# A two-layer decode kernel: which part of w2 is loaded last, what stays in memory between the layers, and the block order at the turn

## The chip, the cores and the metric

One core of one Trainium2 chip runs the whole kernel, in float32. The metric is the time of one execution on the device in microseconds (us); lower is better. The engines of the core work side by side: TensorE (PE, with its weight loads PEld) multiplies, VectorE (DVE) and ScalarE (ACT) work on single elements, SyncE (SP) issues nearly all the transfers from the chip's main memory (HBM) into the on-chip memory, and 16 DMA engines carry them out. A transfer of 128 rows is shared by the 16 DMA engines, and counts as landed when the last of them is done with its part.

## The reference

```python
def A(x, k_cache, v_cache, wq, wo):            # attention over a cache, 8 sequences, one new token each
    q = (x @ wq) as 32 heads of 128            # wq 1024 x 4096
    k, v = caches of 4 heads x 4096 x 128      # each one serves 8 query heads
    p = softmax(q @ k.T * 128 ** -0.5)
    return (p @ v as 4096 columns) @ wo        # wo 4096 x 1024

def B(x, w1, b1, w2, b2):                      # w1 1024 x 3584, w2 3584 x 1024
    return gelu(x @ w1 + b1) @ w2 + b2

for layer in range(2):                         # the same weights and caches in both layers
    x = x + A(layernorm(x), ...)
    x = x + B(layernorm(x), ...)
```

x is 8 x 1024. The caches are 64 MB each (8 MB of K and 8 MB of V for one sequence), wq and wo 16 MB each, w1 and w2 14 MB each. Both layers need all of it, and the on-chip memory holds only a part.

## The kernel before

The on-chip buffer, the arena, is 52 units of 0.5 MB (`SCW` = 1024 columns of 128 rows each, 4 bytes). A list `stream` holds all loads in the order in which SP issues them, each with its size in units and the unit at which it starts, all written out by hand. `pump` issues loads from the head of the list as long as their units are free; `release` frees units and calls `pump`. A load that has to wait holds back all those behind it. In the program, the load waits for the last instruction that reads its units.

The order of the work in a layer: the query product (wq), then for each sequence K (scores, in 8 pieces of 1 MB), softmax, V (8 pieces of 1 MB), then wo, a layernorm, w1 with gelu (7 groups of 512 hidden columns, `expand`), and w2. Layer 0 takes the sequences 0 to 7, layer 1 takes them 7 to 0, so the last V pieces of sequence 7 can stay in the arena from one layer to the next (`n_kept`). wq stays in the arena during the whole attention of layer 0 (all but its last row block, which is parked elsewhere, in part in `spare`, and comes back with `unpark`; a small rest is loaded again as "qe").

**The turn** from layer 0 to layer 1 is `swap`. w2 is cut into column blocks (`W2_PARTS`). For one block, `down` multiplies all 28 row blocks of 128 hidden columns (28 x 2 TensorE passes, since a float32 matmul is issued as two), VectorE copies the sum, small matmuls turn it (L511), and the result is added to x. These columns of x then are the rows by which wq is multiplied for the next layer (`q_part`, 8 passes for each 1 MB of wq). Used wq tiles free their units, and w2's next blocks and the first K pieces of layer 1 go there. So the chain is: w2 block, copy, wq parts, release, next load. Most of w2 stays in the arena for layer 1, except for its last four row blocks (`LAST` = 24 and on): of these two column blocks of 256 stay, and the other two are loaded again.

**The end** is layer 1's `expand` with `work`: after each group of w1 the product with the w2 rows of the group before is done (`grow`, `down_row`). The last four row blocks need the last group of w1. The list ends with w1's pieces (five of 2 MB, three of 1 MB, then 0.5, 0.25 and 0.25 MB) and the two column blocks of the last four rows of w2, 1 MB, in five parts (`LATE`); one part is cut into rows (`ROWS`), so the last seven transfers have 16 to 256 KB. After the last matmul, VectorE adds the sum to x (L835), and SP stores x.

Of the kernel before, what the change touches and what calls it, by code (L numbers as in the profile page):

```python
# [38 lines left out]
UNPARK = 14  # L39
# [8 lines left out]
LATE_ORDER = [(e, c) for e in range(4) for c in range(CB)]  # L48
# [60 lines left out]
def decode_layers(ctx: ExitStack, tc: tile.TileContext, x, kc, vc, wq, wo, w1, w2, out):  # L109
# [145 lines left out]
    def pump():  # L255
        while stream:
# [8 lines left out]
            for r0, r1 in ROWS.get(key, ((0, P),)):  # L265
                nc.sync.dma_start(out=slot.ap[r0:r1, 0:src.shape[1]], in_=src[r0:r1])
# [18 lines left out]
    def expand(name, rs, work=None):  # L285
        n = 0
        for slot in tiles((name,)):
# [23 lines left out]
            release(slot)  # L311
            if n % NT:
                continue
            if u < WIDE:
                row = row_s if work or u % 2 else qz[:, P:P + CH]
                nc.scalar.activation(row, acc, AF.Copy, scale=rs)
                if not work:
                    flush()
                pending.append(lambda u=u, row=row: hidden_wide(u, row))
            else:  # L320
                if not work:
                    flush()
                row, hid = row_s[:, 0:P], qz[:, P:2 * P]
                if direct:
                    row = acc[:, 0:P]
                else:
                    nc.scalar.activation(row, acc[:, 0:P], AF.Copy, scale=rs)
                nc.vector.transpose(hid, row)
                hv = hid.rearrange("p (t q) -> p t q", t=GT)[:, :, 0:B]
                if biased:  # L330
                    hidden_group(u, None, hv)
                else:
                    hidden_group(u, lambda pre: nc.vector.tensor_tensor(pre, hv, bias1(u), ALU.add))
            for f in (work or {}).get(u, ()):
                f()
# [15 lines left out]
    def q_part(acc, u, kt, c0, ap):  # L351

        n = ap.shape[1]
        for j in range(4):
            d0, d1 = max(c0, j * CH), min(c0 + n, (j + 1) * CH)
            if d0 < d1:
                nc.tensor.matmul(acc[u][32 * j:32 * j + 32, d0 - j * CH:d1 - j * CH], xnT[:, kt * XS:kt * XS + 32],  # L357
                                 ap[:, d0 - c0:d1 - c0], start=(kt == 0), stop=(kt == NT - 1 and d1 == (j + 1) * CH))
# [4 lines left out]
    def queries(rs):  # L363
        acc = q_acc()
        at = 0
        for slot in tiles(("q0",)):
            for c in range(0, slot.cols, W):
                q_part(acc, at % 2, at // 2, 0, slot.ap[:, c:c + W])
# [94 lines left out]
    def down_row(y, kts, cs=range(CB)):  # L463

        for kt in kts:
            for c in cs:
                nc.tensor.matmul(y[32 * c:32 * c + 32], h_at(kt), w2_at[c, kt], start=(kt == 0), stop=(kt == NFT - 1))  # L467

    def w2_kts(c, i):

        k0, n, _ = W2_PARTS[c][i]
        return range(k0, k0 + n)

    def arrive(key, kts):
        slot = held[key]
        for e, kt in enumerate(kts):
            w2_at[key[1], kt] = slot.ap[:, e * Q4:(e + 1) * Q4]
        return kts

    def swap():  # L480
# [8 lines left out]
        def used(kt, u):  # L489
# [3 lines left out]
            if (kt, u) == (4, 0):  # L493
                st["unparked"] = unpark()

        for c in range(CB):
            y = ys[:, c % 2 * Q4:(c % 2 + 1) * Q4]
# [5 lines left out]
            slot = held.pop(("w2", c, [k0 for k0, _, _ in W2_PARTS[c]].index(LAST)))  # L503
            if c < len(LATE_AT):
                release(slot)
            ysb = row_s[:, c % 2 * Q4:(c % 2 + 1) * Q4]
# [3 lines left out]
            for i in range(2):  # L510
                nc.tensor.matmul(pt[:, i * B:(i + 1) * B], ysb[:, i * P:(i + 1) * P], bsel, start=True, stop=True)  # L511
            xc = xv[:, 2 * c:2 * c + 2]
# [396 lines left out]
```

## Time and profile before

| | before |
|---|---|
| median of 3 runs | 849.92 us (849.53 to 849.97) |
| the profiled execution | 849.15 us |
| span from first to last instruction in it | 847.4 us |
| read from HBM | 357.78 MB, 422 GB/s over the span |
| TensorE busy | 520.4 us (61%) |
| VectorE busy | 203.1 us (24%) |
| mean granted TensorE clock | 0.813 |

How to read the rows: the page gives busy shares in 40 equal slices, DMA among them; the chain of work that ended last gives, in order of time, a start, a duration and what was at work. Rows of windows give for a stretch its length, then busy time and number of instructions for PE, PEld, DVE, ACT and POOL, then the granted clock, the busy share of the DMA engines and GB/s. Rows of the timeline give start, time, engine, line, operation, output and inputs, shape and count; in brackets, how long the engine had been idle and what ended that.

### The profile page before, as it was taken

The numbers are of one execution on the slowest core, as the hardware profiler recorded it, in microseconds if no ns is written. First come the engines' busy times: TensorE is split into PE (matmuls) and PEld (weight loads), VectorE is DVE, ScalarE is ACT, GpSimd is POOL, SyncE is SP. The second block draws the span as 40 slices with busy tenths as digits, with TensorE's granted clock in tenths as the row PEclk, the third lists the DMA queues.
The fourth block names the chain that finished last, engine by engine and source line by source line (L and its number), as shares of the span: only waits on it lengthen the run. The fifth ranks groups of instructions, "written<-read, shape, count | busy, mean of one in ns | idle before, by whom it ended". The sixth has DMA issues, their size and how long they took to land.

```text
span 847.4 us, 9420 instructions
## 1 busy us (share of the span) xinstructions
PE 520.4 (61%) x4060; PEld 173.3 (20%) x4060; DVE 203.1 (24%) x692; ACT 55.5 (7%) x118; POOL 2.4 (0%) x14
## 2 busy tenths in 40 slices
PE   0756565655656656655678775476646565665777
PEld 0211111111111111122143222121111111112334
DVE  0013141322223131300120242231413222231022
ACT  0110000000000000000211100000000000000021
POOL 0000000000000000000000000000000000000000
PEclk9977788786887868688889988877896878788689
DMA  9999999999999999999999999999999999999997
GB/s 402 420 421 432 433 422 439 427 431 435 419 429 436 428 438 417 429 428 425 427 410 413 424 428 432 432 433 426 437 427 435 429 434 430 427 435 426 423 426 260
DMA packets 20073, 358.52 MB, mean 423 GB/s; under 512 B 2240, under 2 KB 2880, under 8 KB 4416
## 3 DMA queue, kind: packets, MB, share of 16 engines
q1 hardware_dynamic: 19888, 357.77, 99.2%
q8 instruction: 32, 0.52, 0.3%
q10 hardware_dynamic: 144, 0.15, 0.1%
q14 instruction: 9, 0.07, 0.0%
HBM read 357.78 MB, written 0.13 MB: 422 GB/s over the span
## 4 chain that ended last, share of the span: by engine, by line
DMA 75%; PE 21%; DVE 2%; issue 1%; another core or an unknown queue 1%; ACT 0%; SPq 0%; ACTq 0%; DVEq 0%
DMA arena<-in_k_dram 29%; DMA arena<-in_v_dram 21%; DMA arena<-in_w_dram 11%; DMA arena<-in_wo_dram 8%; PE sps L590 8%; PE o_ps L633 7%; DMA arena<-in_wq_dram 5%; PE y L424 1%; PE acc L357 1%; PE sps L461 1%; PE sps L645 1%; PE acc L301 1%; PE sps L467 0%; ACT sps L614 0%
## 5 line engine op out<-in xcount | busy, mean ns | idle before, releaser
L590 PE MATMUL sps<-arena,qz 128*32 128x512 f32 x1024 | 161.9, 775 | 118.5 <-DMA arena<-in_k_dram 117.4
L633 PE MATMUL o_ps<-arena 128*32 128x512 f32 x512 | 84.2, 788 | 51.1 <-DMA arena<-in_v_dram 39.6
L633 PE MATMUL o_ps<-arena,spare 128*32 128x512 f32 x512 | 85.3, 785 | 45.9 <-DMA arena<-in_v_dram 41.3
L590 PEld LDWEIGHTS sps<-arena,qz 128*32 128x32 f32 x1024 | 36.8, 132 | 208.6 <-issue 170.0
L638 DVE SCALAR_TENSOR_TENSOR scr<-o_ps,bits,scr 128x128 f32<-128x128 f32 x192 | 67.4, 351 | 6.8
L424 PE MATMUL y<-arena,oxT 128*32 128x256 f32 x512 | 42.5, 494 | 28.5 <-DMA arena<-in_wo_dram 28.5
L636 DVE TENSOR_SCALAR scr<-o_ps,bits 128x128 f32<-128x128 f32 x64 | 22.4, 351 | 150.4 <-PE o_ps L633 150.4
L645 PEld LDWEIGHTS sps<-bits,scr 128*128 128x128 f32 x128 | 22.3, 219 | 69.5 <-issue 46.9
L357 PE MATMUL acc<-arena,oxT 128*32 128x512 f32 x248 | 30.5, 630 | 6.0 <-DMA arena<-in_wq_dram 4.6
L633 PEld LDWEIGHTS o_ps<-arena 128*32 128x32 f32 x512 | 16.3, 131 | 83.0 <-issue 47.7
L301 PE MATMUL acc<-arena,oxT 128*32 128x512 f32 x160 | 25.5, 760 | 12.6 <-DMA arena<-in_w_dram 12.6
L633 PEld LDWEIGHTS o_ps<-arena,spare 128*32 128x32 f32 x512 | 17.6, 131 | 76.4 <-issue 51.1
L595 DVE TENSOR_SCALAR_CACHE_REDUCE arena<-sps 128x512 f32<-128x512 f32 x16 | 11.1, 692 | 88.9 <-PE sps L590 88.9
L646 DVE TENSOR_TENSOR oxT<-sps,scr 128x8 f32<-128x8 f32 x64 | 10.6, 165 | 88.9 <-PE sps L645 88.9
L595 DVE TENSOR_SCALAR_CACHE_REDUCE spare<-sps 128x512 f32<-128x512 f32 x16 | 11.1, 692 | 80.8 <-PE sps L590 80.8
L614 ACT ACTIVATE sps<-arena,bits 128x512 f32<-128x512 f32 x16 | 10.9, 681 | 284.3 <-DVE scr L608 284.3
L424 PEld LDWEIGHTS y<-arena,oxT 128*32 128x32 f32 x512 | 19.2, 138 | 49.7 <-DMA arena<-in_wo_dram 28.7
L614 ACT ACTIVATE sps<-spare,bits 128x512 f32<-128x512 f32 x16 | 10.9, 681 | 268.9 <-DVE scr L608 268.9
L645 PE MATMUL sps<-bits,scr 128*128 128x8 f32 x128 | 28.2, 293 | 0.0
L604 PE MATMUL sps<-scr,bits 128*128 128x128 f32 x32 | 7.6, 322 | 22.9 <-DVE scr L600 22.9
L461 PE MATMUL sps<-arena,oxT 128*32 128x256 f32 x224 | 15.0, 409 | 3.8 <-DMA arena<-in_w_dram 3.8
L203 PE MATMUL sps<-ident,xb 128*128 128x128 f32 x6 | 1.5, 345 | 24.4 <-DMA xb<-in_x_dram 23.3
(136 smaller groups left out, 251.1 us busy)
## 6 DMA issues: line engine op xcount, KB each, us to landing
arena<-in_v_dram SPq DMA_DIRECT2D x25, 4096.0 KB, 20.6
arena<-in_k_dram SPq DMA_DIRECT2D x21, 4096.0 KB, 21.0
arena<-in_k_dram SPq DMA_DIRECT2D x20, 2048.0 KB, 18.8
arena<-in_w_dram SPq DMA_DIRECT2D x16, 2048.0 KB, 11.8
arena<-in_v_dram SPq DMA_DIRECT2D x11, 2048.0 KB, 20.2
arena<-in_wo_dram SPq DMA_DIRECT2D x8, 2048.0 KB, 16.1
arena<-in_wo_dram SPq DMA_DIRECT2D x3, 4096.0 KB, 23.9
arena<-in_w_dram SPq DMA_DIRECT2D x6, 1024.0 KB, 19.0
```

Source lines behind the costliest of these rows:

```text
L301: nc.tensor.matmul(acc[32 * j:32 * j + 32, :], lhs, slot.ap[:, c:c + CH], start=(kt < 4), stop=(kt >= NT - 4))
L357: nc.tensor.matmul(acc[u][32 * j:32 * j + 32, d0 - j * CH:d1 - j * CH], xnT[:, kt * XS:kt * XS + 32], ap[:, d0 - c0:d1 - c0], start=(kt == ...
L424: nc.tensor.matmul(y[32 * j:32 * j + 32, 0:Q4], lhs[:, n * B:n * B + 32], slot.ap[:, c + j * Q4:c + (j + 1) * Q4], start=(n == 0), stop=(n ...
L461: nc.tensor.matmul(y[32 * g:32 * g + 32], h_at(kt), w2_at[c, kt], start=(n < 4), stop=(n >= NFT - 4))
L590: nc.tensor.matmul(ps[32 * g:32 * g + 32, :], qz[:, c:c + 32], kt[:, g * CH:(g + 1) * CH], start=(j == 0), stop=(j == HKV - 1))
L595: nc.vector.tensor_scalar(st["row", b].ap[:, half * CH:(half + 1) * CH], ps, SCALE, None, op0=ALU.mult, op1=ALU.max, accum_out=st["mx", b] ...
L614: nc.scalar.activation(pp, row[:, h * CH:(h + 1) * CH], AF.Exp, bias=bias, scale=1.0, accum_out=ls[:, h:h + 1])
L633: nc.tensor.matmul(o[32 * g:32 * g + 32, :], s[:, g], v[:, g * CH:(g + 1) * CH], start=(half == 0), stop=(half == NH - 1))
L636: nc.vector.tensor_scalar(r, o[:, 0:P], sel_t[:, 0:1], None, op0=ALU.mult)
L638: nc.vector.scalar_tensor_tensor(r, o[:, t * P:(t + 1) * P], sel_t[:, t:t + 1], r, op0=ALU.mult, op1=ALU.add)
L645: nc.tensor.matmul(po[:, 0:REP], r_s[j % 2], sel_h, start=True, stop=True)
L646: nc.vector.tensor_tensor(oT_v[:, j * REP:(j + 1) * REP, b], po[:, 0:REP], rl_s[b % 2][:, j * REP:(j + 1) * REP], ALU.mult)
```

## The change

- The four last row blocks of w2 all are loaded again at the end: 2 MB in three transfers of 1, 0.5 and 0.5 MB (row blocks 24 and 25, then 26, then 27, all 1024 columns each). They lie in a copy behind w2's image in HBM.
- Seven pieces of the last V (7 MB) stay between the layers, not six. The buffer for wo and w1 in layer 0 is units 42 to 51, and the first loads of layer 1 go to units 16 to 27 (before: 40 to 51 and 14 to 27). The last V of layer 0 comes in transfers of 1, 3 and 4 MB.
- At the turn w2 comes in five column blocks: 128, 256, 256, 256 and 128 columns (`BLOCKS`, in units of 128 columns from column block 0, 2, 4, 6 and 1). wq's row blocks are stored and used in the order `ORDER`, so that the row block that was parked (now 1) belongs to the last column block. In layer 1 the first quarter of the columns therefore is in two pieces, and `down_row` makes two matmuls of 128 columns there where it made one of 256.
- w1's pieces in layer 1 are six of 2 MB and two of 1 MB. `expand` can take pieces that hold one group's end and the next one's start, which layer 0 needs for its pieces of 2, 2 and 1 MB.
- In one V transfer of sequence 1 in layer 1 (4 MB) the last 64 columns are left out and come in five transfers of 96, 12, 10, 6 and 4 rows (`CUTS`). `ROWS` is gone.

```diff
-UNPARK = 14
+UNPARK = 16
-W2_PARTS = (((0, 16, 40), (16, 8, 44), (LAST, 4, 46)), ((0, 4, 47), (4, 16, 48), (20, 4, 46), (LAST, 4, 0)),
-            ((LAST, 4, 1), (0, 16, 2), (16, 8, 6)), ((LAST, 4, 0), (0, 16, 8), (16, 8, 12)))
-LATE_AT = 14, 15
-LATE = ((0, 0, 2), (1, 0, 2), (0, 2, 2), (1, 2, 1), (1, 3, 1))
-ROWS = {("late", 0, 0): ((0, 8), (8, 16), (16, P))}
+ORDER = [0, 2, 3, 4, 5, 6, 7, 1]
+BLOCKS = ((0, 1), (2, 2), (4, 2), (6, 2), (1, 1))
+W2_PARTS = (((0, 24, 42), (LAST, 4, 45)),
+            ((16, 8, 50), (0, 16, 46), (LAST, 4, 45)),
+            ((0, 16, 0), (LAST, 4, 45), (16, 8, 4)),
+            ((0, 16, 6), (16, 8, 10), (LAST, 4, 45)),
+            ((0, 24, 12), (LAST, 4, 15)))
+LATE = ((0, 2, 15), (2, 1, 17), (3, 1, 45))
+CUTS = {(1, ("v", 1, 2, 0)): ((0, 96), (96, 108), (108, 118), (118, 124), (124, 128))}
...
-            for r0, r1 in ROWS.get(key, ((0, P),)):
-                nc.sync.dma_start(out=slot.ap[r0:r1, 0:src.shape[1]], in_=src[r0:r1])
+            n = src.shape[1]
+            full = n - P // 2 if key in CUTS else n
+            nc.sync.dma_start(out=slot.ap[:, 0:full], in_=src[:, 0:full])
+            for r0, r1 in CUTS.get(key, ()):
+                nc.sync.dma_start(out=slot.ap[r0:r1, full:n], in_=src[r0:r1, full:n])
...
             for c in cs:
-                nc.tensor.matmul(y[32 * c:32 * c + 32], h_at(kt), w2_at[c, kt], start=(kt == 0), stop=(kt == NFT - 1))
+                at = 0
+                for i, w in W2_OF[c] if kt < LAST else ((c, Q4),):
+                    nc.tensor.matmul(y[32 * c:32 * c + 32, at:at + w], h_at(kt), w2_at[i, kt],
+                                     start=(kt == 0 and at == 0), stop=(kt == NFT - 1))
+                    at += w
...
-        for c in range(CB):
-            y = ys[:, c % 2 * Q4:(c % 2 + 1) * Q4]
+        for c, (k0, nk) in enumerate(BLOCKS):
+            w = nk * P
+            y = ys[:, c % 2 * Q4:c % 2 * Q4 + w]
...
-            for kt in (2 * c, 2 * c + 1):
+            for kt in range(k0, k0 + nk):
...
-    n_kept = 6
+    n_kept = 7
...
+    batch(0, last_b, ((8, 28), (4, 36), (4, 40)), ((2, 44), (6, 28), (8, 34)))
-    weights(("o0",), wo[0], [4, 4, 2, 2, 4, 4, 4, 4, 4], fixed(40, 44, 48, 50, 40, 44, 48, 40, 44))
-    weights(("i0",), w1[0], [4] * 7, fixed(48, 40, 44, 48, 40, 44, 48))
+    weights(("o0",), wo[0], [4, 4, 2] * 3 + [2], fixed(*[46, 42, 50] * 3, 46))
+    weights(("i0",), w1[0], [4, 4, 2, 4, 4, 2, 4, 4], fixed(42, 46, 50, 42, 46, 50, 42, 46))
...
-    batch(1, last_b, ((4, 16), (4, 20), (4, 24), (2, 14), (2, 16)), ((4, 20),))
-    batch(1, last_b - 1, ((4, 24), (4, 16), (2, 14), (4, 20), (2, 36)), ((8, 28), (8, 16)))
-    batch(1, last_b - 2, ((4, 36), (4, 24), (8, 28)), ((8, 16), (8, 24)))
-    at = [32, 16, 24] * (4 * B)
+    batch(1, last_b, ((2, 18), (4, 20), (4, 24), (2, 16), (2, 18), (2, 20)), ((2, 22),))
+    batch(1, last_b - 1, ((4, 24), (4, 16), (4, 20), (4, 28)), ((8, 34), (8, 18)))
+    at = [26, 34, 18] * (4 * B)
...
-    weights(("i1",), w1[0], [4] * 5 + [2] * 3 + [1, 0.5, 0.5], fixed(32, 36, 16, 20, 24, 28, 30, 32, 34, 35, 36))
-    for c, e, n in LATE:
-        at = (c * NFT + LAST + e) * Q4
-        to = LATE_AT[c] * SCW + e * Q4
-        stream.append((("late", c, e), 0 if e else 1, w2[0][:, at:at + n * Q4], arena.ap[:, to:to + n * Q4] if e else (LATE_AT[c],), ()))
+    weights(("i1",), w1[0], [4] * 6 + [2] * 2, fixed(34, 38, 18, 22, 26, 30, 34, 36))
+    for e, n, at in LATE:
+        c0 = W2_FROM[-1] + e * D
+        stream.append((("late", e), n, w2[0][:, c0:c0 + n * D], (at,), ()))
...
-            for c, e, n in LATE:
-                arrive(("late", c, e), range(LAST + e, LAST + e + n))
-            for e, c in LATE_ORDER:
-                grow((LAST + e,), (c,))
+            for e, n, _ in LATE:
+                slot = held[("late", e)]
+                for i in range(n):
+                    for c in range(CB):
+                        w2_at[c, LAST + e + i] = slot.ap[:, i * D + c * Q4:i * D + (c + 1) * Q4]
+                grow(range(LAST + e, LAST + e + n))
...
-    return w.reshape(NFT, P, CB, Q4).transpose(1, 2, 0, 3).reshape(1, P, -1)
+    a = w.reshape(NFT, P, D).transpose(1, 0, 2)
+    parts = [a[:, :, k * P:(k + n) * P].reshape(P, -1) for k, n in BLOCKS]
+    return _np.concatenate([*parts, a[:, LAST:].reshape(P, -1)], 1)[None]
```

More of the change, by code (lines that the diff above doesn't have):

```diff
@@ L310, in expand @@
                     f()
[L311 to L325, printed above, removed]
-                else:
[L327 to L335, printed above, removed]
+                if c + CH >= slot.cols:
+                    release(slot)
+                if n % NT:
+                    continue
+                if u < WIDE:
+                    row = row_s if work or u % 2 else qz[:, P:P + CH]
+                    nc.scalar.activation(row, acc, AF.Copy, scale=rs)
+                    if not work:
+                        flush()
+                    pending.append(lambda u=u, row=row: hidden_wide(u, row))
+                else:
+                    if not work:
+                        flush()
+                    row, hid = row_s[:, 0:P], qz[:, P:2 * P]
+                    if direct:
+                        row = acc[:, 0:P]
+                    else:
+                        nc.scalar.activation(row, acc[:, 0:P], AF.Copy, scale=rs)
+                    nc.vector.transpose(hid, row)
+                    hv = hid.rearrange("p (t q) -> p t q", t=GT)[:, :, 0:B]
+                    if biased:
+                        hidden_group(u, None, hv)
+                    else:
+                        hidden_group(u, lambda pre: nc.vector.tensor_tensor(pre, hv, bias1(u), ALU.add))
+                for f in (work or {}).get(u, ()):
+                    f()
         assert n == NGR * NT
@@ L502, in swap @@
                 n += len(kts)
[L503 to L506, printed above, removed]
+            release(held.pop(("w2", c, [k for k, _, _ in W2_PARTS[c]].index(LAST))))
+            ysb = row_s[:, c % 2 * Q4:c % 2 * Q4 + w]
             nc.vector.tensor_copy(ysb, y)
@@ L525, in swap @@
                         spot.free()
+                        next(stats, None)
                     else:
@@ L530, in swap @@
                         slot.free()
-                    if c == CB - 1 and (kt, u) in ((NT - 2, 1), (NT - 1, 0)):
                         next(stats, None)
```

51 lines of the change are left out of this document (28 added, 23 removed).

## The prediction

> **What bounds the kernel now.** I read the page first, then the chain of work that ended last, then the last stretch and the middle of the run in small windows.
>
> ```profile
> span 847.4 us, 9420 instructions
> ...
> DMA  9999999999999999999999999999999999999997
> GB/s 402 420 421 432 433 422 439 427 431 435 419 429 436 428 438 417 429 428 425 427 410 413 424 428 432 432 433 426 437 427 435 429 434 430 427 435 426 423 426 260
> ...
> q1 hardware_dynamic: 19888, 357.77, 99.2%
> q8 instruction: 32, 0.52, 0.3%
> ...
> DMA 75%; PE 21%; DVE 2%; issue 1%; another core or an unknown queue 1%; ACT 0%; SPq 0%; ACTq 0%; DVEq 0%
> ```
>
> The load queue is never idle: 357.77 MB, 0.9 in every slice but the last. Time can come from four places only: fewer bytes, a queue that runs dry, engines that are held up by something else, and what follows the last byte. Slices 21 and 22 (410 and 413 GB/s) hold the turn between the layers; the last slice holds the end. The chain there:
>
> ```profile
> 819.48 20.66 DMA arena<-in_w_dram
> ...
> 840.19 0.43 PE acc L304 x8
> 840.62 3.55 PE sps L467 x54
> ...
> 844.19 0.42 DVE xb L835
> ```
>
> So w1's last piece lands at 840.15, and TensorE alone then takes 4.0 us to the last VectorE add. The same end by windows (the last three columns are the granted TensorE clock, the busy share of the DMA engines and GB/s):
>
> ```profile
> 834.00:835.00 1.00, 1.00 (x46) 1.00 (x42) 0.79 (x5) 0.23 (x1) 0.00 (x0) 1.00 1.12 420
> 835.00:836.00 1.00, 1.00 (x32) 0.73 (x26) 0.53 (x3) 0.00 (x0) 0.00 (x0) 1.00 1.02 274
> ...
> 838.00:839.00 1.00, 1.00 (x39) 0.70 (x28) 0.00 (x0) 0.00 (x0) 0.00 (x0) 1.00 0.92 256
> ...
> 841.00:842.00 1.00, 1.00 (x20) 0.65 (x20) 0.76 (x4) 0.23 (x1) 0.00 (x0) 1.00 0.61 217
> 842.00:843.00 1.00, 1.00 (x23) 0.63 (x22) 0.00 (x0) 0.00 (x0) 0.00 (x0) 1.00 0.13 39
> ...
> 845.00:846.00 1.00, 0.00 (x0) 0.00 (x0) 0.00 (x0) 0.00 (x0) 0.00 (x0) 1.00 0.38 131
> ```
>
> Two things are to be seen. The data ends at 842.2 (39 GB/s is a sixth of the rate before), about 2 us before the last add. And from 835 on the rate is 250 to 274, six tenths of 420: some six of the sixteen engines have nothing left while about ten still have some seven us of work. A transfer counts as landed when its slowest engine is done, so these ten set the end. What holds single engines up can be seen in one place, the 2.5 us from 828.5 on, with one instruction fetch in them:
>
> ```profile
> q8 instruction: 1, 0.02, 2.6%
> ```
>
> 2.6% of 16 engines' 2.5 us is 1.04 us on one engine. There are 32 such fetches. Spread over ten engines that is an estimate of about 3 us each, so much of the seven us is fetches that fell on the same engines.
>
> **The change part by part.**
>
> *Bytes.* Seven pieces of V are kept rather than six: 1 MB less. Four row blocks of w2 come again for all 1024 columns (2 MB) rather than for 512 (1 MB): 1 MB more. wq, wo, w1, K and w2 at the turn are the same to the byte. Net 0. w2's image gets 4096 more columns, so its rows lie 131,072 bytes apart rather than 114,688. wo's rows lie 131,072 apart already:
>
> ```profile
> 377.00:398.00 21.00, 13.02 (x160) 5.71 (x154) 0.00 (x0) 0.00 (x0) 0.00 (x0) 0.76 1.00 424
> ```
>
> That window is wo at 424 GB/s, the usual rate: **0**. [...] The trace speaks for 0.
>
> *The end.* TensorE's rows:
>
> ```profile
> 833.44 1.95 PE L304 MATMUL acc<-arena,spare 128*32 128x128 f32 x64
> ...
> 840.43 3.71 PE L467 MATMUL sps<-arena,oxT 128*32 128x256 f32 x56
> ...
> 844.19 0.42 DVE L835 TENSOR_TENSOR xb<-xb,sps 128x256 f32<-128x256 f32 x1 [2.23 <-PE sps L467]
> 844.64 0.35 SPq L837 DMA_DIRECT2D out_dram<-xb  x1
> ```
>
> A wide pass (256 columns) costs 3.71/56 = 66 ns, a narrow one (128) 1.95/64 = 30 ns. Before, 56 passes stand behind w1's last piece: 24 for row blocks 21 to 23, 32 for the late ones. After, w1's last piece lands with 2 MB behind it in the queue. The work it releases is 32 narrow passes (0.98), row blocks 21 to 23 (3 x (6 wide + 4 narrow) = 1.5) and the first late pair (16 wide, 1.06): 3.6 us. The 2 MB take 5.0 us (2.49 us per MB, below), so it is hidden; if it were not, at most the old 3.55 us would come back. What stays bare is the last 0.5 MB: 8 wide passes, 0.53 us after it lands. The output's data, issued at 844.64, is moved in the window 845 to 846 and the span ends soon after it at 847.4, so I add an estimated 0.5 us from last data to landing: 842.2 + 0.5 + 0.53 = 843.2, against 844.14 (840.43 + 3.71). **-0.9 us**; bounds 0 (TensorE late again) and -1.4 (no receipt delay).
>
> *Piece sizes at the end.* Seven late transfers of 16 to 256 KB and w1 pieces down to 256 KB become one of 1 MB, two of 0.5 MB and two w1 pieces of 1 MB. Ten sixteenths of 430 would be 269 GB/s and the windows show about 250: at most 7% of 7 us, -0.5; at least 0. I take **-0.2**, nearer to 0 because six of sixteen is itself a rounded count. SP's queue gets shorter there (18 issues become 11, at 0.35 us each), and none of them was late.
>
> *The cut V transfer.* 128 rows by 64 columns (32 KB) leave one 4 MB transfer and come as five small ones: 0.08 us of data at 430 GB/s, SP's five issues while it waits anyway. Bounds 0 and five issue times, 1.7; since only 1/128 of a transfer is involved and about 8 MB are queued around it, **+0.1**.
>
> *The last batch of layer 0.* One 4 MB V transfer now holds the last four pieces, and the buffer for wo and w1 is 10 units of 0.5 MB rather than 12. The rows of V there:
>
> ```profile
> 352.29 3.64 PE L633 MATMUL o_ps<-arena 128*32 128x512 f32 x16 [4.30 <-DMA arena<-in_v_dram]
> ...
> 356.39 2.01 PE L633 MATMUL o_ps<-arena 128*32 128x512 f32 x16
> ...
> 360.51 0.39 PE L645 MATMUL sps<-bits,scr 128*128 128x8 f32 x2
> 362.18 1.93 PE L424 MATMUL y<-arena,oxT 128*32 128x256 f32 x32 [1.28 <-DMA arena<-in_wo_dram]
> ...
> 376.86 3.45 PE L424 MATMUL y<-arena,oxT 128*32 128x256 f32 x32 [3.81 <-DMA arena<-in_wo_dram]
> ```
>
> TensorE waits for the first 2 MB of wo until 362.18, so V, 2 MB ahead of it, landed at about 357.2 (2.49 us per MB, below). It would now need four pieces, 3.64 + 2.01 + 0.5 = 6.2 us, to 363.4 rather than 360.6. The wo piece in units 50 and 51 waits for this, because unit 51 holds the probabilities. 4 MB of wo are queued before it, 10 us from 357.2 to 367.2; 363.4 + 2.0 (issue to data, below) is 365.4: covered by 1.8 us for the slowest engine. In the ring, 3 MB (7.5 us) stay queued while a 2 MB piece is used for at most 3.45 + 2.0: covered by 2. **0**; bounds 0 and +1.
>
> *The turn.* Five blocks instead of four; Two of them, and a quarter of w2 in layer 1, go in narrow passes: 56 passes more here and 48 more there, with the columns unchanged. What matters is the chain block, VectorE copy, small transposes, wq parts, release, next load.
>
> ```profile
> 430.97 2.98 PE L304 MATMUL acc<-arena,oxT 128*32 128x128 f32 x64 [2.36 <-DMA arena<-in_w_dram]
> 435.87 4.52 PE L461 MATMUL sps<-arena,oxT 128*32 128x256 f32 x56 [1.92 <-DMA arena<-in_w_dram]
> 441.04 0.58 PE L511 MATMUL sps<-bits,scr 128*128 128x8 f32 x4 [0.65 <-DVE scr L507]
> 441.89 3.64 PE L357 MATMUL acc<-arena,oxT 128*32 128x512 f32 x32 [0.27 <-DVE oxT L513]
> ...
> 465.78 1.07 PE L461 MATMUL sps<-arena,oxT 128*32 128x256 f32 x16 [0.22 <-DMA arena<-in_w_dram]
> ...
> 476.10 5.31 PE L590 MATMUL sps<-arena,qz 128*32 128x512 f32 x32 [1.10 <-DVE oxT L546]
> ```
>
> The queue's pace: 14 MB of w2 between 430.9 and 465.7, 2.49 us per MB. Where it ran thin before, a load was issued by SP at 442.98, and the rate fell and came back:
>
> ```profile
> 443.50:444.00 0.50, 0.50 (x8) 0.13 (x4) 0.00 (x0) 0.00 (x0) 0.00 (x0) 1.00 0.92 336
> ...
> 444.50:445.00 0.50, 0.50 (x12) 0.20 (x8) 0.00 (x0) 0.00 (x0) 0.00 (x0) 1.00 0.67 221
> 445.00:445.50 0.50, 0.50 (x12) 0.18 (x8) 0.00 (x0) 0.00 (x0) 0.00 (x0) 1.00 1.00 377
> ```
> ```profile
> 442.98 2.08 SPq L266 DMA_DIRECT2D arena<-in_w_dram  x3
> ```
>
> so 2.0 us from issue to data, and only the early engines were idle. After: block 0 starts at 435.87 (gelu sets that), 56 narrow passes at 2.98/64 = 47 ns take 2.6, to 438.5; copy and transposes 1.1; two wq parts 2 x 0.91 (3.64/4) to 441.4; data of the next load from 443.4. Queued by then are 5.25 MB behind w1, to 444.0: covered by 0.6 for the slowest engines, not for those ahead. Block 1 ends near 445.3, its first wq part near 447.7, data from 449.7, against 449.0 + 1.2 = 450.2 (the 2 MB and 0.5 MB before it): covered by 0.5. Then the loads of K: the parts of wq that free units 20 to 23 are used near 466, data from 468, against 465.7 + 2.5 (the 1 MB K piece that goes first) = 468.2: covered by 0.2. The last block is 56 narrow passes and two wq parts instead of four, but TensorE comes to it only near 468, so the first scores stay near 476. **0** for the slowest engines; bounds -0.5 (scores earlier) and +1.5 (0.5 at each thin place).
>
> *What the thin places do to the engines ahead.* They lose up to 1.5 us of lead, and a fetch that falls on them later makes them the slowest. Bounds 0 (the fetch falls into their idle time) and +1.04 (one fetch). I take the middle, **+0.5**.
>
> Sum: -0.9 - 0.2 + 0.1 + 0 + 0 + 0.5 = -0.5 us on the profiled execution's 849.15 (span 847.4 and 1.75 around it): 848.65. The median of the runs is 849.92, 0.77 higher, so **849.4**, 0.06% less. About 0.2% (1.7 us) is what can be told from no change.
>
> **The rivals.**
>
> *Drawn level.* The engines lose their lead and the fetch falls on one in full, with no gain from piece sizes: -0.9 + 0.1 + 1.04 = +0.2, 850.1. For it: the thin places are three where there was one.
>
> *One fetch fewer on the slowest engines.* The changed instruction count (about 200 more) moves the fetches against the loads; if one of the late engines is spared, -1.04, with the full gain from pieces: -0.9 - 0.5 + 0.1 - 1.04 = -2.3, 847.6. Against it: more instructions mean more fetches.
>
> *The turn runs dry (slower).* The place is the first load behind block 0, where 0.6 us cover it. If TensorE is granted the lower clock there, the wq parts cost twice as much (L633 shows 3.64 for what else takes 1.92): +1.8, and block 0 +0.8 (56 x 2 x 30 ns), 2.0 us dry, and 1 more at the next two places: -0.5 + 3 = +2.5, 852.4. It decides once the chain is more than 0.6 + 2.2 us late. Speaking for it and against it:
>
> ```profile
> 441.00:466.00 25.00, 21.75 (x264) 9.06 (x268) 1.38 (x5) 3.16 (x2) 0.00 (x0) 1.00 1.01 404
> ```
>
> TensorE is 87% busy in the turn, so nothing catches up; but its granted clock is 1.00 there.
>
> *Rows 131,072 bytes apart.* If that spacing halved the rate of w2's 16 MB, it would add 16 x 2.49 = 40 us, 889. Against it stands wo's row above.
>
> **How the numbers follow.** The sum as it stands 0.45, drawn level 0.24 (both within 0.2%), one fetch fewer 0.16 (faster), dry 0.14 and row spacing 0.01 (slower): faster 0.16, same 0.69, slower 0.15. The range goes from 848.1, the ends that gain (-1.4 - 0.5 + 0.1), to 851.7, the dry case with 2.3 us dry rather than 3; it leaves out about 2 in 10, and the likeliest case alone is 848.6 to 850.1.
>
> **What would show it.** End: the last L467 group of 8 passes with a wait on a load ahead of it, and the add within 1 us of the last landing; if L467 runs on without a wait, TensorE was the bound. Turn: the rate by half microseconds near 443, 449 and 468, low but not zero, and first scores near 476. Engines: the stretch of about 250 GB/s at the end gets shorter if they are drawn level. Layer 0's end: the first wo piece for units 50 and 51 issued near 363. I am wrong if a window of 1 us shows no data, if first scores come after 478, or if the last load lands more than 1.5 us away from 842.7.

## The result, and the profile after

| | before | after |
|---|---|---|
| median | 849.94 us (849.53 to 850.67) | 860.01 us (856.76 to 861.38) |
| ratio | | 1.0112, interval [1.0082, 1.0142] |
| the profiled execution | 849.15 us | 859.56 us |
| its span | 847.4 us | 857.8 us |

The change makes the kernel 10.1 us slower; 849.4 was predicted, in a range up to 851.7. The page of the changed kernel:

```profile
span 857.8 us, 9631 instructions
...
GB/s 397 420 430 429 429 425 427 435 423 434 426 429 438 424 435 425 418 380 396 417 397 348 382 415 435 432 430 431 432 432 431 431 427 431 433 426 433 419 426 290
...
q1 hardware_dynamic: 19472, 357.77, 98.5%
q8 instruction: 33, 0.54, 0.2%
```

The bytes are the same to the last digit, as predicted. What fell is the rate, in six or seven slices from the end of layer 0's attention to the start of layer 1's. The same by windows (length, busy times, then granted clock, DMA share, GB/s), first before:

```profile
50.00:340.00 290.00, 171.03 (x1044) 47.73 (x1044) 73.96 (x241) 10.63 (x28) 0.00 (x0) 0.77 1.00 430
352.00:398.00 46.00, 29.49 (x312) 12.19 (x312) 4.62 (x16) 0.00 (x0) 0.00 (x0) 0.80 1.01 426
398.00:431.00 33.00, 20.21 (x196) 7.52 (x189) 8.19 (x40) 8.27 (x17) 0.00 (x0) 0.84 1.01 428
431.00:466.00 35.00, 29.22 (x384) 13.59 (x388) 3.72 (x16) 3.98 (x5) 0.63 (x1) 0.90 1.01 408
466.00:500.00 34.00, 25.06 (x184) 7.83 (x176) 12.86 (x44) 3.76 (x8) 0.20 (x1) 0.85 1.00 424
520.00:790.00 270.00, 166.99 (x1066) 52.02 (x1070) 71.54 (x230) 9.11 (x24) 0.00 (x0) 0.79 1.00 431
```

Then after, each window moved with its stage:

```profile
50.00:340.00 290.00, 175.19 (x1044) 48.95 (x1044) 74.05 (x241) 10.63 (x28) 0.00 (x0) 0.74 1.00 429
352.00:398.00 46.00, 28.89 (x288) 11.10 (x280) 4.62 (x16) 0.00 (x0) 0.00 (x0) 0.73 0.95 388
398.00:435.00 37.00, 20.01 (x204) 7.37 (x200) 8.06 (x39) 8.26 (x17) 0.00 (x0) 0.91 1.00 410
435.00:476.00 41.00, 31.25 (x410) 15.04 (x414) 4.32 (x19) 3.99 (x5) 0.63 (x1) 0.92 0.95 372
476.00:510.00 34.00, 23.64 (x202) 8.51 (x198) 11.56 (x41) 3.76 (x8) 0.20 (x1) 0.80 0.99 397
520.00:790.00 270.00, 168.47 (x1036) 51.33 (x1036) 74.98 (x241) 10.63 (x28) 0.00 (x0) 0.78 1.00 431
```

Attention runs at 429 to 431 GB/s in both. A window's shortfall in time is its length times (427 - rate)/427, where 427 stands for the undisturbed rate of these stages. Before: 0.1, -0.1, 1.6, 0.2. After: 4.2 in the last V and wo, 1.5 in w1, 5.3 at the turn, 2.4 at the first K and V of layer 1. That is 13.4 against 1.8: 11.6 us, of which the end of the kernel gives about half a microsecond back (below). Rounding of the rates to 1 GB/s leaves 0.1 us in each window.

**Where the queue ran dry.** Three places can be seen in TensorE's and SP's rows. First the last V and the wo piece for units 50 and 51:

```profile
357.69 3.64 PE L646 MATMUL o_ps<-arena 128*32 128x512 f32 x16 [3.97 <-DMA arena<-in_v_dram]
...
361.78 2.68 PE L646 MATMUL o_ps<-arena 128*32 128x512 f32 x16
...
364.71 1.93 PE L433 MATMUL y<-arena,oxT 128*32 128x256 f32 x32
...
393.40 6.01 PE L433 MATMUL y<-arena,oxT 128*32 128x256 f32 x64 [1.27 <-DMA arena<-in_wo_dram]
```
```profile
364.54 26.27 SPq L272 DMA_DIRECT2D arena<-in_wo_dram  x8
397.10 11.37 SPq L272 DMA_DIRECT2D arena<-in_w_dram  x4
```

The first row is TensorE's wait of 3.97 us for 4 MB of V in one transfer. Its 32 passes then take until 364.5, and only then does SP issue the wo piece, 364.54. Its data come 2 us later, and until then the DMA engines run out one after the other (windows of one microsecond; the rate falls, but never to zero):

```profile
364.00:365.00 1.00, 1.00 (x18) 0.50 (x14) 0.42 (x2) 0.00 (x0) 0.00 (x0) 1.00 0.50 213
365.00:366.00 1.00, 1.00 (x24) 0.61 (x20) 0.93 (x4) 0.00 (x0) 0.00 (x0) 1.00 0.82 172
...
397.00:398.00 1.00, 1.00 (x20) 0.33 (x10) 0.00 (x0) 0.00 (x0) 0.00 (x0) 0.75 0.16 66
```

By the trace's completion events (each transfer of 128 rows reports 16 times, once for each DMA engine) the slowest DMA engine lost 1.5 us here and the fastest 2.7. The 1.5 us are one engine's: fifteen of the sixteen events of this transfer lie within 0.91 us, the last comes 2.38 us after the first. Second, at 397: w1's first 2 MB piece waits for the first 32 of the 64 passes from 393.40 until 397.10, 3.7 us, while only two wo pieces of 1 MB each are queued ahead of it. The slowest engine lost 1.2, the fastest 2.4. From there on the engines, before up to 3.6 us apart, are 0.5 us apart. Third, the turn:

```profile
444.24 1.07 PE L470 MATMUL sps<-arena,oxT 128*32 128x256 f32 x16
448.85 3.95 PE L470 MATMUL sps<-arena,oxT 128*32 128x256 f32 x40 [3.53 <-DMA arena<-in_w_dram]
453.36 0.61 PE L524 MATMUL sps<-bits,scr 128*128 128x8 f32 x4 [0.56 <-DVE scr L520]
454.24 2.78 PE L366 MATMUL acc<-arena,oxT 128*32 128x512 f32 x24 [0.27 <-DVE oxT L526]
```
```profile
449.00:450.00 1.00, 1.00 (x12) 0.45 (x12) 0.00 (x0) 0.00 (x0) 0.00 (x0) 0.50 1.00 426
...
453.00:454.00 1.00, 0.61 (x4) 0.52 (x4) 0.30 (x1) 0.00 (x0) 0.00 (x0) 1.00 0.55 107
454.00:455.00 1.00, 0.76 (x8) 0.29 (x12) 0.17 (x1) 0.00 (x0) 0.00 (x0) 1.00 0.64 184
```

TensorE waits 3.53 us for the second block's 2 MB, is granted half the clock (0.50 from 448.70 to 452.12), and takes 3.95 us for 40 passes (99 ns each against 67 at full clock in the row above them). A piece of 0.5 MB is issued when they are done, at 452.87. The next load, 1 MB, has to wait for the first wq parts too: it is issued at 455.37, 5.3 us after the block's last piece landed (450.06), and 2 us later there is data again. These rows are of one execution; two kernels below show that the dry place at the turn moves from block to block.

**What came as predicted** is the end:

```profile
853.83 0.64 PE L478 MATMUL sps<-arena,oxT 128*32 128x256 f32 x8 [0.61 <-DMA arena<-in_w_dram]
854.53 0.42 DVE L851 TENSOR_TENSOR xb<-xb,sps 128x256 f32<-128x256 f32 x1 [3.78 <-PE sps L478]
```

The last group is 8 passes behind a wait on a load. The last landing is at 853.79 and the add starts 0.74 us later; before, it was 842.81 and 1.38.

### The profile page after: what moved, and what is told of

It reads as the page before. It is cut to its first block, busy times and chain, and to the rows that moved or that the text cites. A ratio compares the mean times of both kernels' runs of the same rounds, so it can differ in the third digit from the quotient of the medians.

```text
span 857.8 us, 9631 instructions
## 1 busy us (share of the span) xinstructions
PE 531.8 (62%) x4164; PEld 181.4 (21%) x4164; DVE 203.3 (24%) x694; ACT 55.5 (6%) x118; POOL 2.4 (0%) x14
## 3 DMA queue, kind: packets, MB, share of 16 engines
q1 hardware_dynamic: 19472, 357.77, 98.5%
## 4 chain that ended last, share of the span: by engine, by line
DMA 74%; PE 22%; DVE 2%; issue 1%; another core or an unknown queue 1%; ACT 0%; SPq 0%; ACTq 0%; DVEq 0%
DMA arena<-in_k_dram 29%; DMA arena<-in_v_dram 23%; DMA arena<-in_w_dram 12%; PE sps L603 8%; PE o_ps L646 8%; DMA arena<-in_wo_dram 6%; DMA arena<-in_wq_dram 5%; PE y L433 1%; PE sps L470 1%; PE acc L366 1%; PE sps L658 1%; PE acc L309 0%; PE acc L312 0%; ACT sps L627 0%
## 5 line engine op out<-in xcount | busy, mean ns | idle before, releaser
L603 PE MATMUL sps<-arena,qz 128*32 128x512 f32 x1024 | 167.2, 799 | 116.1 <-DMA arena<-in_k_dram 115.7
L646 PE MATMUL o_ps<-arena 128*32 128x512 f32 x512 | 90.5, 839 | 51.3 <-DMA arena<-in_v_dram 39.8
L470 PE MATMUL sps<-arena,oxT 128*32 128x256 f32 (+1 forms) x280 | 15.7, 366 | 6.6 <-DMA arena<-in_w_dram 6.6
```

Of the source, the lines that this page charges most:

```text
L470: nc.tensor.matmul(y[32 * g:32 * g + 32], h_at(kt), w2_at[c, kt], start=(n < 4), stop=(n >= NFT - 4))
L603: nc.tensor.matmul(ps[32 * g:32 * g + 32, :], qz[:, c:c + 32], kt[:, g * CH:(g + 1) * CH], start=(j == 0), stop=(j == HKV - 1))
L646: nc.tensor.matmul(o[32 * g:32 * g + 32, :], s[:, g], v[:, g * CH:(g + 1) * CH], start=(half == 0), stop=(half == NH - 1))
```

## The experiments

They take the change apart (the end alone; six kept pieces with the five blocks; four blocks with the seven kept pieces) and mend the dry places one by one. The times of the kernels whose queue runs dry scatter widely (the changed kernel over 4.6 us, others up to 11), while the kernel before stays within 2.2 us; so differences of 1 to 2 us between such kernels are read from their profiles, not from their medians. All shortfalls are worked out as above, in the windows of after (for the end alone those of before, for six kept pieces its own).

| kernel | median us | profiled us | V, wo | w1 | turn | layer 1 start |
|---|---|---|---|---|---|---|
| before | 849.9 | 849.2 | 0.1 | -0.1 | 1.6 | 0.2 |
| after | 860.0 | 859.6 | 4.2 | 1.5 | 5.3 | 2.4 |
| no cut V transfer | 860.8 | 853.9 | 3.9 | 1.2 | 3.0 | 0.8 |
| V halves | 858.4 | 856.8 | 2.3 | 1.7 | 5.7 | 0.8 |
| and ring | 856.7 | 856.0 | 1.5 | 1.1 | 4.9 | 0.9 |
| and parts | 855.4 | 854.5 | 1.2 | 0.8 | 5.2 | 1.0 |
| TensorE kept busy | 859.0 | 859.6 | 4.3 | 2.2 | 5.2 | 2.3 |
| end alone (+1 MB) | 850.0 | 850.2 | 0.1 | 0 | 1.6 | 0.2 |
| six kept, five blocks (+1 MB) | 853.2 | 852.3 | 0 | 0.1 | 3.5 | 0 |
| seven kept, four blocks | 858.4 | 857.2 | 3.0 | 1.9 | 6.4 | 0.6 |

### The cut V transfer

```diff
-CUTS = {(1, ("v", 1, 2, 0)): ((0, 96), (96, 108), (108, 118), (118, 124), (124, 128))}
+CUTS = {}
```

> The changed kernel without the cut V transfer (that 4 MB come whole). Theory (the load queue runs dry at the end of layer 0 and at the turn): the cut has no part in it, 859.5 to 860.5 us, like the changed kernel's 860.0. Rival (five small transfers, which hold five of the eight places for transfers in flight, throw the loads of the last two sequences back): most of the 10 us comes back, 851 to 853.

860.83 (853.92 to 864.71), ratio 1.0121 [1.0073, 1.0169]. By the medians nothing of the loss comes back. With 11 us between two executions of this one kernel, the times alone would not exclude an effect of a few us; but in the changed kernel's trace the cut transfer is issued near 713 us, far behind the dry places, in a stretch that runs at 431 GB/s in both kernels.

Up to there this program is the changed kernel, so its trace shows the same loads a second time:

```profile
435.00:476.00 41.00, 32.53 (x444) 15.21 (x437) 4.98 (x23) 3.99 (x5) 0.63 (x1) 0.92 0.98 396
```

Here half the clock was granted at block 0 and its wq parts (0.5 from 440.28 to 447.11). TensorE came late to the second block, did not wait for it, and the 1 MB load behind it was issued 3.2 us after the block's last landing, not 5.3. The turn loses 3.0 us instead of 5.3, all four stages 8.9 instead of 13.4, and the execution takes 853.9 us instead of 859.6.

### The last V in two transfers of 2 MB

```diff
-... ((2, 44), (6, 28), (8, 34)))
+... ((2, 44), (6, 28), (4, 34), (4, 38)))
```

> The changed kernel with the last four V pieces of layer 0 in two transfers of 2 MB instead of one of 4 MB. Theory: the dry place at 365 to 367 us, where the 1 MB wo piece for units 50 and 51 waits until the last V pieces are used (issued at 364.5), goes away, because two of the four pieces are used 5 us earlier; the slowest engine gains 1.5 us there, 858 to 859 in all, and what the engines ahead keep of their lead may give another 1 us. Rival (the loss is in the ring and the turn alone): 860 as before.

858.37 (856.75 to 860.13), ratio 1.0102 [1.0084, 1.0119], in the theory's range. The wo piece is issued at 359.12 instead of 364.54 and the first dry place is gone: the shortfall in V and wo falls from 4.2 to 2.3. What is left of it is mostly the second place, where w1's first piece is issued at 395.11 and the fastest DMA engine loses 2.1 us. The turn, unchanged in this program, ran differently again: the second block waits 1.07 us and goes at full clock (2.37 us for its 40 passes), the third waits 2.81 us, the mean granted clock from 435 to 476 is 0.92, as in the changed kernel, and the shortfall is 5.7 all the same.

### And smaller pieces in the ring of wo and w1

```diff
-weights(("i0",), w1[0], [4, 4, 2, 4, 4, 2, 4, 4], fixed(42, 46, 50, 42, 46, 50, 42, 46))
+weights(("i0",), w1[0], [2, 4, 2, 4, 4, 2, 4, 2, 4], fixed(48, 42, 50, 46, 42, 50, 46, 50, 42))
```

(w2's first blocks move to the units that come free first.)

> As the one with V in halves, and w1 of layer 0 in pieces of 1, 2, 1, 2, 2, 1, 2, 1, 2 MB in another order of places, so that 3 MB rather than 2 MB are in the queue when the first 2 MB piece of w1 waits for wo's last 2 MB piece to be used; the first and second column block of w2 change places. Theory: the second dry place (399 to 402 us) goes too, w1's last piece in layer 0 lands at 431 to 432 instead of 435.4, and the time is 854.5 to 857. Rival (the ring of 10 units is too small in any order): w1's end stays at 434 or later, 858 or more.

856.69 (855.51 to 863.35), ratio 1.0097 [1.0062, 1.0133]. The time is in the theory's range; w1's last piece lands at 432.57 (after: 435.43, before: 430.93), a little behind the 431 to 432 that the theory gave. So the first two places explain about 3 us of the 10, by the medians as by the landing; the intervals of the two kernels overlap, so this is a rough size. What remains is the turn and what follows it.

### TensorE kept busy at the turn

```diff
                 down(y, c, kts, n)
                 n += len(kts)
+                if (c, i) == (1, 0):
+                    for e in range(24):
+                        nc.tensor.matmul(pt[...], h_at(0), w2_at[1, 16 + e % 8], start=True, stop=True)
```

> The changed kernel with 48 added TensorE passes, whose results nothing uses, in the second column block at the turn, where TensorE waits 3.5 us for w2 and is then granted half its clock. Theory (half the clock there lengthens the chain from w2's last part to the next release, which is what runs the queue dry at 456 to 458): the clock stays at 1.00, the next 40 passes take 2.4 us instead of 4.0, the load behind them is issued 1.6 us earlier, and the time falls by 1.5 to 3 us, to 857 to 858.5. Rival (the order of the blocks alone makes the place dry): 860, and the load is issued as late as before.

859.0 (857.53 to 866.91), ratio 1.0127 [1.0086, 1.0169]. Inconclusive by its own design. The 40 passes did go at full clock:

```profile
448.67 2.80 PE L520 MATMUL sps<-arena,oxT 128*32 128x256 f32 x48
451.26 2.37 PE L470 MATMUL sps<-arena,oxT 128*32 128x256 f32 x40
```

but the extra 48 passes held TensorE until 451.3, after the 2 MB had landed at 449.82. So the 1 MB load came 5.1 us after the block's last landing instead of 5.3. Half the clock was granted in this execution too, but at block 0 (0.5 from 442.08 to 445.49), whose 56 narrow passes took 3.03 us; in the changed kernel they took 1.97.

### And smaller w2 parts

```diff
-W2_PARTS = (((0, 24, 46), (LAST, 4, 49)),
-            ((16, 8, 50), (0, 16, 42), (LAST, 4, 49)),
+W2_PARTS = (((0, 8, 46), (8, 16, 47), (LAST, 4, 49)),
+            ((16, 8, 50), (0, 8, 42), (8, 8, 44), (LAST, 4, 49)),
```

> The kernel of the ring experiment (V's last in halves, w1 of layer 0 with smaller pieces so that 3 MB stay queued) and, at the turn, the first block's 24 row blocks as 8 and 16, and the second block's (0, 16) of 2 MB as two of 1 MB, so that TensorE never waits over 2.5 us there. Theory (TensorE waits 3.5 us for the 2 MB part, is then granted half the clock for 3.4 us, and needs 4 us for 40 passes that stand between the landing and the next issue): the 40 passes no longer stand behind one landing, the next w2 piece is issued some 2 us earlier (450 to 451 instead of 452.6), and the time is 854.0 to 855.5. Rival (the loss at the turn comes from engines drawn level and from fetches, whatever TensorE does): 856 to 857.

855.44 (854.46 to 858.14), ratio 1.0070 [1.0051, 1.0090], just inside the theory's range, with an interval that reaches into the rival's; the kernel it was made from had 856.69. The place is mended: 8 passes stand behind the block's last landing, and the next piece is issued at 448.95, not 452.59, 3.2 us after that landing. But the next place fails in its stead:

```profile
445.76 0.64 PE L470 MATMUL sps<-arena,oxT 128*32 128x256 f32 x8 [0.19 <-DMA arena<-in_w_dram]
...
456.79 1.93 PE L470 MATMUL sps<-arena,oxT 128*32 128x256 f32 x16 [3.32 <-DMA arena<-in_w_dram]
458.50 1.80 PE L366 MATMUL acc<-arena,oxT 128*32 128x512 f32 x8
```

TensorE, now early, waits 3.32 us for the third block, takes 121 ns for each of the 16 passes behind that wait (67 at full clock), and the load behind them is issued at 460.37, so late that the fastest DMA engine loses 3.3 us and the slowest 1.0. Of 3.6 us gained at one block, 1.5 reach the end in the profiled executions (856.0 and 854.5); the turn's shortfall stays at 5.

### The end alone

```diff
-LATE_AT = 14, 15
-LATE = ((0, 0, 2), (1, 0, 2), (0, 2, 2), (1, 2, 1), (1, 3, 1))
-ROWS = {("late", 0, 0): ((0, 8), (8, 16), (16, P))}
+LATE = ((0, 2, 14), (2, 1, 0), (3, 1, 1))
...
-... [4] * 5 + [2] * 3 + [1, 0.5, 0.5], fixed(32, 36, 16, 20, 24, 28, 30, 32, 34, 35, 36))
+... [4] * 5 + [2] * 4, fixed(32, 36, 16, 20, 24, 28, 30, 32, 34))
```

> The kernel before with the changed end alone: all four last row blocks of w2 loaded last in three transfers, w1's end in 1 MB tiles; four column blocks at the turn, six MB of V kept and the rings of layer 0 stay as before. It reads 1 MB more than either kernel (2.45 us at 429 GB/s), since the space that the change uses for a seventh MB of V stays unused. Theory (the end does what the prediction said and everything lost was lost before it): 849.9 + 2.45 - 0.7 = 851.4 to 851.9, and 0.6 to 0.9 us from the last landing to the last add instead of 1.4. Rival (the end gains nothing by itself): 852.3 or more, still 1.4 us after the last landing.

850.02 (849.57 to 852.39), ratio 1.0009 [0.9999, 1.0018]. It reads 1 MB more than the kernel before and costs next to nothing for it: the end is worth more than the theory had.

```profile
844.55 0.64 PE L463 MATMUL sps<-arena,oxT 128*32 128x256 f32 x8 [0.54 <-DMA arena<-in_w_dram]
845.26 0.42 DVE L831 TENSOR_TENSOR xb<-xb,sps 128x256 f32<-128x256 f32 x1 [3.25 <-PE sps L463]
```

From wo's last landing to the add it takes 40.2 us (805.10 to 845.26), before 39.5 (804.74 to 844.19) with 1 MB less, that is 2.45 us of data: a gain of 1.7. 0.6 of that is the interval from last landing to add. The remaining 1.1 are in the stretch of the small pieces: in the kernel before, two loads there with an instruction fetch beside them (829.51 and 838.46) cost the slowest DMA engine 0.6 and 0.4 us. In this kernel the fetches at 831.33 and 838.83 cost it nothing; one beside wo, ahead of the stretch, cost 0.6. So nearly all of the 1.1 is fetches that fell on other engines, and not the size of the pieces. In the changed kernel the same interval is 41.4, a gain of 0.5, with fetches of 0.3 and 0.9 us in it. So the end is worth 0.5 to 1.7 us, by whether a fetch falls on the slowest engine.

### Six kept pieces with the five blocks

```diff
-    n_kept = 7
+    n_kept = 6
...
+W2_PARTS = (((0, 24, 40), (LAST, 4, 43)),
+            ((16, 8, 44), (0, 16, 48), (LAST, 4, 46)),
+            ((0, 4, 47), (LAST, 4, 43), (4, 16, 0), (20, 4, 4)),
+            ((0, 16, 5), (16, 8, 9), (LAST, 4, 46)),
+            ((0, 24, 11), (LAST, 4, 43)))
```

(The lists of wo and w1 are those of before.)

> The changed kernel with six MB of the last V kept instead of seven, so that wo, w1 and the turn have twelve units of 0.5 MB again, and the places of wo and w1 of layer 0 as before; the five column blocks, the narrow first block and the changed end stay, the cut of the V transfer is left out. It reads 1 MB more than either kernel, as the kernel with the changed end alone does. Theory (twelve units instead of ten are what kept the queue full; the five blocks cost little): 850.0 to 852.5, no window without data before the turn, and w1's last piece lands near 431 instead of 435.4. Rival (the narrow first block, its order or the narrow passes are the cause, whatever the space): 855 or more, with the rate at the turn as low as in the changed kernel.

853.19 (852.29 to 854.92), ratio 1.0046 [1.0032, 1.0060]: between the theory's range and the rival's. Its windows:

```profile
352.00:398.00 46.00, 30.23 (x296) 11.70 (x300) 4.62 (x16) 0.00 (x0) 0.00 (x0) 0.72 1.01 427
398.00:433.00 35.00, 23.74 (x268) 10.84 (x260) 8.44 (x41) 8.36 (x18) 0.00 (x0) 0.84 1.01 426
433.00:472.00 39.00, 30.22 (x412) 14.18 (x408) 4.41 (x20) 3.89 (x5) 0.63 (x1) 0.96 0.97 389
472.00:506.00 34.00, 25.65 (x180) 8.11 (x184) 14.80 (x51) 3.76 (x8) 0.20 (x1) 0.85 1.01 427
```

With twelve units, wo, w1 and layer 1's start are as before. The five blocks still cost: against the end alone (same bytes, same twelve units, four blocks) this is +3.2 us. The row that shows it is the second block again:

```profile
442.98 4.01 PE L470 MATMUL sps<-arena,oxT 128*32 128x256 f32 x40 [2.51 <-DMA arena<-in_w_dram]
```

### Seven kept pieces with four blocks

```diff
-ORDER = [0, 2, 3, 4, 5, 6, 7, 1]
-BLOCKS = ((0, 1), (2, 2), (4, 2), (6, 2), (1, 1))
+ORDER = list(range(8))
+BLOCKS = ((0, 2), (2, 2), (4, 2), (6, 2))
+W2_PARTS = (((0, 16, 46), (16, 8, 50), (LAST, 4, 42)),
+            ((0, 12, 43), (LAST, 4, 42), (12, 12, 0)),
+            ((0, 16, 4), (LAST, 4, 42), (16, 8, 8)),
+            ((0, 16, 10), (16, 8, 14), (LAST, 4, 42)))
```

(On top of the V halves and the ring.)

> The kernel of the ring experiment (seven MB of the last V kept, the changed end, V's last in halves, w1 of layer 0 in smaller pieces) with four column blocks of 256 at the turn in the order of the kernel before, in the same ten units: 3 MB of the first block and then 2 MB of the second are queued before wq's first 4 MB come free. Theory (the narrow first block, which frees 2 MB of wq where a wide one frees 4, and the waits of 3.5 us on 2 MB pieces make the turn run dry; keeping a seventh MB of V need not): the turn costs what it costs before, up to 1 us more, and the bytes and the end of the change remain: 849.5 to 851.5, and w2's last lands 34 to 36 us after w1's last, as before. Rival (ten units instead of twelve are too few whatever the blocks): the queue runs dry after the first or second block and it stays at 854 to 857.

858.38 (856.47 to 865.13), ratio 1.0117 [1.0090, 1.0145], above even the rival's 854 to 857. The rival stands: in ten units, four wide blocks run dry too, after the first block (448 to 451) and after the second:

```profile
448.00:449.00 1.00, 1.00 (x13) 0.26 (x9) 0.00 (x0) 0.00 (x0) 0.00 (x0) 1.00 0.37 131
449.00:450.00 1.00, 1.00 (x16) 0.39 (x12) 0.00 (x0) 0.00 (x0) 0.00 (x0) 1.00 0.60 115
...
461.00:462.00 1.00, 1.00 (x8) 0.20 (x4) 0.00 (x0) 0.00 (x0) 0.00 (x0) 0.50 0.21 33
```

Here w1's last piece lands at 435.69, though the loads up to there are those of the ring experiment (432.57): thin covers make the same list land 3 us apart.

### Sixteen more instruction fetches

```diff
         nc.tensor.matmul(po[:, 0:REP], r_s[j % 2], sel_h, start=True, stop=True)
+        for e in range(16):
+            nc.tensor.matmul(po[32 * (e % 4):32 * (e % 4) + 32, P:P + 1], neg_m, sums["r0"], start=True, stop=True)
```

> The kernel before with 16 more tiny matmuls, whose result nobody reads, in each of the 64 steps that put the heads' outputs in place: some 4,000 more TensorE instructions, so 16 more fetches of 16 KB beside the 32 that there are, and nothing else in the transfers. Theory (each fetch holds one of eight data engines for some 1.5 us, which the slowest engine adds up): two more for each of the eight engines, 2 x 1.55 = 3.1 us, 852.5 to 853.5. Rival (fetches cost nothing that the end shows, since the other engines' lead or the queue takes them up): 849.9 to 850.5. Above 854 would say that the extra matmuls themselves cost time on TensorE.

852.62 (852.28 to 854.40), ratio 1.0037 [1.0022, 1.0051]: +2.9 us for 16 fetches, 0.18 us each, in the theory's range.

```profile
PE 551.5 (65%) x6108; PEld 197.7 (23%) x6108; DVE 203.1 (24%) x692; ACT 55.6 (7%) x118; POOL 2.4 (0%) x14
...
q8 instruction: 48, 0.79, 0.4%
```

TensorE's 12,216 instructions make 48 fetches of 16 KB (before: 8,120 and 32), so one for about 254. A part of the 2.9 us could be a thinner turn, where this kernel's trace shows 1.5 us lost behind a load; that part wasn't separated.

## Why the prediction was wrong

The sum was -0.5; +10.1 came. By its own steps:

- **Bytes, row spacing, cut transfer: right.** 357.77 MB. The kernel with the end alone has w2's rows 131,072 bytes apart too, and its turn runs at 407 GB/s, the turn before at 408. No loss at the cut transfer.
- **The end: right in kind.** -0.9 and -0.2 were predicted, -0.5 measured in the changed kernel and -1.7 in the kernel with the end alone; what lies between them is fetches, so neither size is a hit. The predicted last landing, 842.7, came at 853.79 for what was lost earlier.
- **The last batch of layer 0, "0; bounds 0 and +1": wrong twice.** "It would now need four pieces ... to 363.4" took the old rows 3.64 and 2.01; V landed 0.4 us later, at 357.55, and the second 16 passes took 2.68, granted half the clock (0.50 from 356.55 to 363.37): 364.5. The cover of 1.8 us had been measured against the slowest engine alone; the fastest was 3.6 us ahead and fell dry by 2.7, and in levelling the engines this place and the next used up the lead that hides later delays: three of w1's loads behind them cost the slowest engine 0.8, 0.5 and 0.4 us, where all of w1 cost it 0.3 in the kernel before. "In the ring, 3 MB (7.5 us) stay queued" is wrong where wo ends and w1 begins: ahead of w1's first 2 MB piece stand two of 1 MB, 5.0 us, against a use of 3.7 + 2.0 ("at most 3.45 + 2.0" was nearly right). Measured in the two stages: 5.7 us of shortfall on the mean engine, and 2.7 at these two places on the slowest; by the medians about 3 of the 10 come back when both are mended.
- **The turn, 0 for the slowest engines with bounds of -0.5 and +1.5: wrong.** Block 1 was to end "near 445.3", 1.3 us after its last piece; its passes ended 2.7 us after that landing, since the full clock of the trace before was carried over to a chain with a new 3.5 us wait in it. This wait, on a 2 MB piece with only 16 passes to do before it, is not in the working at all. The third rival, "the turn runs dry", named the lower clock and its doubled prices, but put it at the first load behind block 0, where the slowest engine lost nothing, and gave it +3 and a chance of 0.14. What happened in the profiled execution was this mechanism one block later, at +3.7 on the mean engine (5.3 against 1.6); in the traces of other kernels it came at block 0 or at the third block as well. So the rival had the mechanism, at a wrong place and too small.
- **Engines ahead, +0.5 with bounds of 0 and +1.04: too small.** It allowed for one fetch. By completion events the slowest engine's losses add up to 17.2 us after and 6.3 before; after the levelling, single loads with a fetch beside them cost it 2.2 (issued at 457.08, in the turn), 0.8 and 0.9. The 2.2 are more than the 1.5 or so by which a fetch sets an engine back elsewhere; the rest is unexplained.
- **The start of layer 1, "covered by 0.2": wrong.** The first of its late loads, 2 MB of K for units 20 to 23, is the one that the working took up; with the turn late it was issued at 475.11, and the DMA engines lost 1.1 to 1.4 us. Two K loads of 1 MB behind it (487.38 and 489.08), which the working leaves out, cost the fastest engine 0.5 and 0.6. The stage's shortfall is 2.4 us; with six pieces kept it is 0.
- **The signs.** Of the three signs of being wrong two came: first scores at 485.80, not by 478, and the last load at 853.79. The third did not: no window of a microsecond at the changed kernel's dry places is without data, and the lowest has 66 GB/s.

The experiments split the loss in two. Against the end alone, five blocks cost 3.2 us (853.2 to 850.0) in twelve units. The seventh kept piece, with the rings and block places in ten units that go with it, costs 860.0 - 853.2 = 6.8 us although it saves 1 MB, 2.45 us: 9.3 us. Blocks and units don't simply add, since four blocks in ten units are no better (858.4). What stays open is how much of the turn's loss is the clock and how much the space: the experiment for it spent what it gained. Half the clock at the second block alone is not needed for the loss, since the V halves lose 5.7 us at the turn with that block at full clock. None of these kernels is faster than the kernel before; the end alone equals it.

## What to carry to other kernels

When a buffer is made smaller, work out what is still queued ahead of each single load at the moment when it is issued, for the DMA engine that is furthest ahead and with TensorE's prices at the lower clock (here 99 ns a pass, not 67); a mean ("3 MB in the ring") hides the one place that has 2. The stretch of the trace before that ran at full clock gave no prices for a version with a new wait of 3.53 us in it. When one dry place is mended, look for the next before counting the gain.

## What the runs showed of the hardware

**Instruction fetches cost time in this kernel, which is bound by loads.** Sixteen more cost 2.9 us, 0.18 us each at most, and TensorE's 12,216 instructions made 48 fetches of 16 KB, one for about 254. The fetch packets of the kernel before take 1.07 us each in the mean. Its completion events show what they do to the loads: the wq transfer that landed before the first fetch has its sixteen events within 0.40 us; after TensorE's first eight fetches, at 305 us, seven lie within 0.56 us and nine come 1.52 to 1.88 us after the first, one more with each fetch and one with a fetch of another queue; the ninth fetch (330.72) falls on an engine that is late already, and its event comes 3.27 us after the first. After twelve fetches, in the transfer whose first event comes at 403.05, still nine are late, and four of these by 3.1 to 3.4 us. So in this trace the first twelve fetches go round eight of the sixteen engines, each costs its engine about 1.5 us, and a transfer is complete only when the last engine is.

**Half the clock was granted behind waits of 2.51 and 3.53 us at the turn.** In the changed kernel it was granted from 448.70 to 452.12, and the 40 passes behind the wait of 3.53 us took 99 ns each. In the kernel with six kept pieces the wait was 2.51 us: the 40 passes behind it took 4.01 us, 100 ns each, and half the clock was granted from 443.54 to 446.95.

```profile
443.00:444.00 1.00, 1.00 (x16) 0.62 (x20) 0.00 (x0) 0.00 (x0) 0.00 (x0) 0.77 1.07 434
444.00:445.00 1.00, 1.00 (x13) 0.43 (x8) 0.00 (x0) 0.00 (x0) 0.00 (x0) 0.50 1.14 475
```

**The kernels with many dry places had unsteady times.** The kernel before stays within 2.2 us over all its runs (848.67 to 850.88) and the end alone within 2.8; the kernels in ten units scatter over 3.4 to 10.8 us in 4 to 6 runs each. The two traces of one program up to 713 us, the changed kernel and the one without the cut, differ by 4.5 us of shortfall and 5.6 us of time.
